# A gated recurrence with a fast-multiplied feed-forward block: how many items of the down product a unit with stored h rows gives out

## The chip, the cores and the metric

The kernel runs on one core of one Trainium2 chip. The metric is device time in microseconds (us) of one execution; smaller is better. Engines: PE is TensorE's matmul side and PEld its weight loads, DVE is VectorE, ACT is ScalarE, POOL is GpSimd, and SP's queue issues most DMAs.

## The reference

```python
S, D, H, Dh, F = 2048, 576, 32, 18, 4608
xn = layernorm(x)
s  = hedgehog_linear_attention(xn, wqkv, w_phi) @ wo
g  = silu(xn @ w_gate)                    # S x F
u  = xn @ w_up                            # S x F
y  = (g * u) @ w_down                     # S x D
out = x + s * silu(y)
```

All is in float32. The attention part comes first in the kernel; the change lies in the last part, the feed-forward block, which takes two thirds of the time.

## The kernel before

**Split operands.** Each float32 operand is held as two parts, hi and lo (`split`, lines 57 to 59: a cast on ACT, a subtraction on DVE), and a product is three matmuls: hi by hi, hi by lo, lo by hi. This is why every prepared operand costs one ACT and one DVE instruction.

**Units.** F = 4608 is cut in 36 blocks f of 128. The token rows are done in two halves, pass 0 (i = 0) and pass 1 (i = 1). A unit (i, n) works on one f of one pass and yields an h block, two tiles of 128 x 512: `ha` (seven buffers) and `hb` (six). In 30 units of each pass, `gate_up` (line 591) computes h from the X operands with seven products of seven matmuls each (128 x 512, line 570), into the PSUM tiles `px`, `py` and `pw`, combined by Strassen's sums. For the other six f, 0 to 5, h was computed in the attention phase and lies in DRAM (`h_dram`); such a unit runs `stored` (line 583), which only loads `ha` and `hb` through SP's queue. Stored units stand at n = 1, 5, 9, 13, 17, 21 in pass 0 and at n = 0, 4, 8, 12, 16, 20 in pass 1.

**The down product.** Four units in a row (n = 4m to 4m + 3) make a group of two pairs. After the third, `strassen` (line 730) puts two steps in a queue, p1 and p7; after the fourth, five more: p4, p5, p6, p2, p3. A step has a preparation (`prep`, line 799: some POOL sums, then two `hh` splits of h rows and two `dw` splits of down weights) and two items. An item (line 785) is 12 matmuls of 128 x 288 (line 669) into one of two PSUM buffers `pd`, then the evacuation, one addition on DVE into a sum tile (line 794; a copy on ACT, line 792, for the first group). The sum tiles have the names `acc`, `X` and `sx`. At the end of a pass two last f pairs are done directly (`plain`), in items of 12 matmuls as well.

**fill and look.** `gate_up` calls `fill` after four of its products, `stored` calls it too. A call gives out items from the head of the queue until `share` units of work (2, later 3) are given; an item of a group with two pairs counts 2, so a call normally gives one. It gives none if no more than `LAG` = 3 units of work are queued. `look` prepares steps up to two ahead. `stored`'s items run with no product of its own between them, and, as one call of `gate_up` comes after its last product, that item stands right before them.

The number of items by unit, worked out from this code, for a middle group of pass 0 and of pass 1 (st is the stored unit; the queue in units of work at the unit's end in brackets):

| pass 0 | n = 7 | n = 8 | n = 9 st | n = 10 |
|---|---|---|---|---|
| before | 4 (22) | 4 (14) | 4 (6) | 2 (10) |

| pass 1 | n = 7 | n = 8 st | n = 9 | n = 10 |
|---|---|---|---|---|
| before | 4 (22) | 4 (14) | 4 (6) | 2 (10) |

At n = 10 the next group's p1 and p7 enter the queue at the unit's end. The four items of n = 9 in pass 0 are the second item of p5, both of p6 and the first of p2; those of n = 10 are the second of p2 and the first of p3. In the stored unit n = 1 of pass 0 the queue is empty. In the first stored unit of pass 1 the calls give out the last items of pass 0.

**Order.** The program text fixes dependences and priorities. A planner, the tile scheduler, orders the instructions on each engine when the program is built, by priority and by its own model of when each will be ready, so an engine's order is near the text's but not the same. At run time each engine follows that fixed order and waits where an operand or a buffer isn't ready.

**Loads.** In pass 0 gate-up weights are loaded raw, split, and written to `w_dram`; in pass 1 the split weights are loaded from there (line 546), each into a buffer that a product of the unit before has freed. At the start of pass 1 the seven X operands are loaded anew (`operands`).

Of the kernel before, what the change touches and what calls it, by code (L numbers as in the profile page):

```python
# [46 lines left out]
def gated_hedgehog_kernel(ctx: ExitStack, tc, x, w_qk, w_v, w_phi, wo, w_gu, w_tail, w_down, ident_in, mask_in, out):  # L47
# [527 lines left out]
    def h_tile():  # L575
        return [fp.tile([P, BT], F32, name=n, bufs=b) for n, b in (("ha", 7), ("hb", 6))]
# [6 lines left out]
    def stored(src, fill):  # L583
        h = h_tile()
        for r in range(2):
            nc.sync.dma_start(h[r], src[:, r * BT:(r + 1) * BT])
        for _ in range(4):
            fill()
        return h

# [255 lines left out]
    def fill(lag=LAG):  # L846
        done = 0
        while queue and done < share[0] and (sum(c for q in queue for c, _ in q[2]) > lag or not queue[0][0]):
            look()
            c, item = queue[0][2].pop(0)  # L850
            item()
            done += c
            if not queue[0][2]:
                queue.pop(0)
# [15 lines left out]
    for i, n, f in units:  # L870
# [3 lines left out]
        if f >= EARLY:  # L874
# [3 lines left out]
            if todo and (i, f) != (0, NF - 1):  # L878
                ready.append(gate_up_weights(*todo.pop(0)))
        h = stored(h_dram[i, f], fill) if f < EARLY else gate_up(w, xo, fill, (i, f) == (0, EARLY))  # L880
        if n % 2 == 0:
            g = {"f": (f, units[units.index((i, n, f)) + 1][2]), "h": [h]}
# [58 lines left out]
```

## Time and profile before

| | |
|---|---|
| median of 3 runs | 1654.41 us (1653.33 to 1656.06) |
| the profiled execution | 1654.66 us, of which the span of instructions is 1652.9 us |
| attention phase and h rows for f below 6 | 0 to about 545 us |
| pass 0 | about 545 to 1086 us |
| pass 1 | about 1086 to 1640 us |
| granted TensorE clock | 0.999 |

In the rows of the profile, L669 PE is an item's matmuls, L570 PE a gate-up product's, L59 DVE the lo half of a split, L58 ACT the hi half, L794 DVE an item's evacuation, L586 SP the loads in `stored`. A timeline row has start, length, engine, line, operation, tiles and shapes and count, and in brackets the engine's idle time before it and what released it. Ends of matmuls are modelled, so time lost on PE is best taken from start to start.

### The profile page before, as it was taken

The page shows a single profiled execution, that of the slowest core. Times are in us where ns is not written, and L with a number is a line of the kernel's source. Part 1 is how long each engine was busy: PE and PEld are TensorE (multiplying, and loading weights), DVE is VectorE, ACT ScalarE, POOL GpSimd, SP SyncE. Part 2 cuts the span into 40 slices and gives each one's busy share as a digit, 9 for nine tenths or more (in the row PEclk, how much of TensorE's full clock was granted, in tenths as well). Part 3 has the DMA queues.
Part 4 walks back from the last instruction along what each step waited for, and adds up shares of the span by engine and source line. Part 5 has one row for each costly group of instructions (what it writes and reads, how often), then busy time and mean ns, then how long its engine had stood idle before and what let it go on. Part 6 is the DMA issues. An engine that isn't in the chain of part 4 may idle for free.

```text
span 1652.9 us, 25205 instructions
## 1 busy us (share of the span) xinstructions
PE 1614.8 (98%) x9441; PEld 1434.1 (87%) x9441; DVE 1175.4 (71%) x1722; ACT 715.7 (43%) x1389; POOL 622.1 (38%) x660
## 2 busy tenths in 40 slices
PE   6999999999999999999999999999999999999998
PEld 5899998999987688888888888888888888888887
DVE  7678758899852477887787777845567667566578
ACT  5533345444431455445444444445433333433334
POOL 3467500343202444554554453422333234133132
PEclk9999999999999999999999999999999999999999
DMA  8623313343218545445445444495444556556435
GB/s 284 215 77 109 109 34 111 94 141 109 73 47 306 182 159 190 158 167 186 161 171 185 174 173 165 132 355 185 152 137 148 164 182 202 171 178 194 139 114 172
DMA packets 118108, 264.69 MB, mean 160 GB/s; under 512 B 12418, under 2 KB 48386, under 8 KB 116194
## 3 DMA queue, kind: packets, MB, share of 16 engines
q1 hardware_dynamic: 107628, 247.44, 44.9%
q0 software_dynamic: 3072, 11.02, 2.4%
q10 hardware_dynamic: 7286, 4.63, 0.9%
q8 instruction: 74, 1.21, 0.3%
q14 instruction: 48, 0.39, 0.1%
HBM read 164.21 MB, written 98.83 MB: 159 GB/s over the span
## 4 chain that ended last, share of the span: by engine, by line
PE 64%; DVE 3%; DMA 1%; issue 1%; POOL 0%; ACT 0%; SPq 0%; DVEq 0%; POOLq 0%
PE px L570 23%; PE pd L669 22%; PE pw L570 11%; PE py L570 6%; PE pe L92 2%; DVE hh L59 1%; DMA ha<-h_dram 1%; DVE acc L641 0%; DVE dw L59 0%; DVE acc L794 0%; DMA X<-s_dram 0%; DMA rb<-in_B_w_down 0%; DVE w L59 0%; DVE X L794 0%; DVE ha L630 0%
## 5 line engine op out<-in xcount | busy, mean ns | idle before, releaser
L669 PEld LDWEIGHTS pd<-dw,hh 128*128 128x128 f32 x3048 | 430.9, 188 | 31.6 <-DVE dw L59 6.4
L669 PE MATMUL pd<-dw,hh 128*128 128x288 f32 x3048 | 448.0, 297 | 8.4 <-DVE dw L59 4.8
L570 PE MATMUL px<-X,w 128*128 128x512 f32 x1440 | 374.8, 394 | 1.8 <-ACT w L58 1.0
L570 PEld LDWEIGHTS px<-X,w 128*128 128x128 f32 x1440 | 261.4, 188 | 55.9 <-ACT s L599 6.1
L570 PE MATMUL pw<-X,w 128*128 128x512 f32 x720 | 186.7, 394 | 0.0
L570 PEld LDWEIGHTS pw<-X,w 128*128 128x128 f32 x720 | 134.0, 189 | 30.2 <-DVE s L604 0.3
L604 DVE TENSOR_TENSOR s<-pw,s 128x512 f32<-128x512 f32 x120 | 82.8, 690 | 105.2 <-ACT s L599 93.4
L92 PE MATMUL pe<-X,wh 128*128 128x512 f32 (+1 forms) x480 | 152.0, 400 | 1.7 <-POOL X L199 0.7
L794 DVE TENSOR_TENSOR acc<-pd,acc 128x576 f32<-128x576 f32 x128 | 96.1, 752 | 72.2 <-PE pd L669 72.0
L599 ACT COPY s<-px 128x512 f32<-128x512 f32 x120 | 70.3, 586 | 156.4 <-PE px L570 156.3
L59 DVE TENSOR_TENSOR hh<-ha,hh 128x512 fp32r<-128x512 f32 x140 | 110.6, 815 | 23.6 <-ACT hh L58 23.0
L58 ACT CAST hh<-ha 128x512 fp32r<-128x512 f32 x140 | 83.1, 620 | 97.2 <-PE pd L669 79.9
L92 PE MATMUL p<-KVWH,X 128*128 128x288 f32 (+1 forms) x640 | 123.6, 298 | 0.9 <-DVE phi L274 0.9
L92 PEld LDWEIGHTS pe<-X,wh 128*128 128x128 f32 (+1 forms) x480 | 88.5, 189 | 19.7 <-DVE h L120 1.5
L766 POOL TENSOR_TENSOR hb<-hb 128x512 f32<-128x512 f32 x34 | 46.1, 1355 | 152.3 <-DVE hb L626 151.8
L92 PEld LDWEIGHTS p<-KVWH,X 128*128 128x128 f32 (+1 forms) x640 | 100.5, 188 | 1.7 <-issue 1.3
L59 DVE TENSOR_TENSOR w<-ld,w 128x512 fp32r<-128x512 f32 (+1 forms) x90 | 76.3, 848 | 34.2 <-ACT w L58 33.2
L753 POOL TENSOR_TENSOR h<-ha,hb 128x512 f32<-128x512 f32 x34 | 45.7, 1344 | 142.6 <-DVE ha L630 101.1
L570 PE MATMUL px<-X,wt 96*128 96x512 f32 x240 | 94.8, 395 | 0.0
L570 PE MATMUL py<-X,w 128*128 128x512 f32 x360 | 93.7, 394 | 0.1
L58 ACT CAST w<-ld 128x512 fp32r<-128x512 f32 (+1 forms) x90 | 49.4, 549 | 83.5 <-POOL ld L560 50.8
L779 POOL TENSOR_TENSOR ha<-ha 128x512 f32<-128x512 f32 x34 | 52.3, 1554 | 80.5 <-DVE hh L59 80.5
(181 smaller groups left out, 3046.9 us busy)
## 6 DMA issues: line engine op xcount, KB each, us to landing
w_dram<-w SPq DMA_DIRECT2D x87, 512.0 KB, 2.8
w<-w_dram SPq DMA_DIRECT2D x87, 512.0 KB, 4.5
wt<-t_dram SPq DMA_DIRECT2D x59, 336.0 KB, 3.4
ld<-in_B_w_gu SPq DMA_DIRECT2D x30, 512.0 KB, 4.4
X<-sum_dram SPq DMA_DIRECT2D x8, 1280.0 KB, 6.6
rt<-in_B_w_down SPq DMA_DIRECT2D x33, 288.0 KB, 3.2
rb<-in_B_w_down SPq DMA_DIRECT2D x33, 288.0 KB, 3.4
w_dram<-w SPq DMA_DIRECT2D x29, 256.0 KB
```

The source lines that it names most:

```text
L58: nc.scalar.copy(hi, src)
L59: nc.vector.tensor_sub(lo, src, hi)
L92: nc.tensor.matmul(ps, l, r, start=n == 0, stop=n == len(pairs) - 1)
L570: nc.tensor.matmul(ps, l, r, start=first and n == 0, stop=last and n == len(mm) - 1, skip_group_check=True)
L599: nc.scalar.copy(t, ps)
L604: nc.vector.tensor_add(t, ps, t)
L669: nc.tensor.matmul(ps, l, r, start=first and n == 0 and m == 0, stop=n == len(hs) - 1 and m == 2, skip_group_check=True)
L753: sub(s, g["h"][0][0], g["h"][0][1])
L766: nc.gpsimd.tensor_add(a21, a21, g["h"][1][1])
L779: sub(a12, a12, g["h"][0][0])
L794: nc.vector.tensor_add(a2, pd[:, :, 0:HALF], a2)
```

## The change

A stored unit calls `fill` twice in place of four times, so it gives out two items where it gave up to four.

```diff
@@ -584,7 +584,7 @@
         h = h_tile()
         for r in range(2):
             nc.sync.dma_start(h[r], src[:, r * BT:(r + 1) * BT])
-        for _ in range(4):
+        for _ in range(2):
             fill()
         return h
```

What is not given out stays in the queue for the calls that follow. By the same counting as above, items and queue become:

| pass 0 | n = 7 | n = 8 | n = 9 st | n = 10 |
|---|---|---|---|---|
| after | 4 (22) | 4 (14) | 2 (10) | 4 (10) |

| pass 1 | n = 7 | n = 8 st | n = 9 | n = 10 |
|---|---|---|---|---|
| after | 4 (22) | 2 (18) | 4 (10) | 4 (10) |

In pass 0 the second item of p6 and the first of p2 move from n = 9 to n = 10. In the first stored unit of pass 1, four items (the last three of the group steps and one of `plain`) are given out in place of six; (1, 1) gives four as before and (1, 2) two where it gave none.

## The prediction

> **What bounds the kernel now.** I read the page first, then who waited for whom on TensorE from 600 us on, then busy time by stretches, and last the timelines around the units that load their h rows.
>
> ```profile
> span 1652.9 us, 25205 instructions
> PE 1614.8 (98%) x9441; PEld 1434.1 (87%) x9441; DVE 1175.4 (71%) x1722; ACT 715.7 (43%) x1389; POOL 622.1 (38%) x660
> PE   6999999999999999999999999999999999999998
> ```
>
> TensorE is busy for 98% of the span. The forecast therefore rests on the few places where it still waits. From 600 to 1056 us, the part of the first pass with a queue to draw on, these are all (us in total, times, longest):
>
> ```profile
> PE pd L669 <- DVE dw L59: 3.3, 3, 1.5
> PE pd L669 <- DVE X L794: 1.9, 4, 0.5
> ```
>
> Busy time by stretches says where they lie. The columns are the length, then PE, weight loads, DVE, ACT and POOL with their counts, the granted clock, and the DMA share and rate.
>
> ```profile
> 600.00:617.00 17.00, 13.74 (x83) 12.08 (x82) 15.75 (x19) 9.27 (x20) 9.96 (x8) 1.00 0.33 104
> 669.38:726.57 57.19, 56.71 (x316) 50.11 (x316) 45.75 (x67) 27.50 (x55) 29.32 (x29) 1.00 0.50 173
> 719.53:726.57 7.04, 6.56 (x50) 6.35 (x48) 6.96 (x11) 2.80 (x6) 4.70 (x4) 1.00 0.60 200
> 726.57:744.42 17.85, 17.85 (x92) 15.33 (x93) 14.79 (x18) 7.87 (x15) 13.43 (x14) 1.00 0.37 122
> 1192.95:1249.58 56.63, 56.63 (x316) 50.15 (x315) 37.88 (x54) 21.51 (x44) 19.25 (x16) 1.00 0.48 147
> 1136.48:1620.00 483.52, 483.52 (x2672) 426.83 (x2670) 316.40 (x458) 187.41 (x370) 150.76 (x124) 1.00 0.52 159
> ```
>
> The third row is a stored unit of pass 0 (n = 9): DVE is busy for 6.96 of 7.04 us there, so DVE ends that stretch, not TensorE. In the gate-up unit behind it (fourth row) DVE has 17.85 - 14.79 = 3.06 us free and TensorE never waits. The last row is nearly all of pass 1: TensorE without an idle moment, its five later stored units included. Four units with a stored one among them take 57.19 us in pass 0 and 56.63 us in pass 1, for the same 316 matmuls: so here a stored unit costs pass 0 about 0.56 us more than it must.
>
> TensorE around that stored unit:
>
> ```profile
> 711.47 1.77 PE L669 MATMUL pd<-dw,hh 128*128 128x288 f32 x12
> 713.08 1.56 PE L570 MATMUL px<-X,w 128*128 128x512 f32 x6
> ...
> 714.71 1.78 PE L669 MATMUL pd<-dw,hh 128*128 128x288 f32 x12
> ...
> 719.53 6.55 PE L669 MATMUL pd<-dw,hh 128*128 128x288 f32 x48
> 726.57 1.82 PE L669 MATMUL pd<-dw,hh 128*128 128x288 f32 x12 [0.48 <-DVE X L794]
> 728.22 1.53 PE L570 MATMUL px<-X,w 128*128 128x512 f32 x6
> ```
>
> One item is 12 matmuls and, from start to start, 713.08 - 711.47 = 1.61 us; the seven matmuls of one gate-up product behind it take 714.71 - 713.08 = 1.63. Five items run in a row, the last of the unit before and the stored unit's four. They need 8.05 us and take 728.22 - 719.53 = 8.69: **0.64 us** are lost (the 0.48 us of idle time is less, because ends of matmuls are modelled). What DVE did meanwhile:
>
> ```profile
> 723.36 0.74 DVE L794 TENSOR_TENSOR acc<-pd,acc 128x576 f32<-128x576 f32 x1
> 724.03 1.72 DVE L59 TENSOR_TENSOR hh<-ha,hh 128x512 fp32r<-128x512 f32 x2
> 725.67 0.75 DVE L794 TENSOR_TENSOR X<-pd,X 128x576 f32<-128x576 f32 x1
> ```
>
> The fifth item needs a pd buffer (there are two), which the third item's addition at 725.67 sets free. That addition stands behind 1.72 us of splits for the next step.
>
> **The change part by part.** It removes the third and fourth call of fill in a stored unit. Nothing is computed less. The two items that these calls gave out go to the next gate-up unit, whose third and fourth calls found the queue at its lag until now; by the code's counts the queue then stands where it stood. (In pass 1 the two items pass through one more unit on the way.) So the change is local: five stored units of pass 0, with 3 items in a row in place of 5, and six of pass 1.
>
> *The four later stored units of pass 0.* The items that waited are the fifth of their runs; they are among those moved, and three in a row need no third evacuation before the products begin. Saved: 4 x 0.64 = 2.6 us. The bounds are 0, if a moved item waits as long at its new place, and 2.6.
>
> *The first of them (n = 5).*
>
> ```profile
> 601.74 3.51 PE L669 MATMUL pd<-dw,hh 128*128 128x288 f32 x25
> 606.17 0.67 PE L669 MATMUL pd<-dw,hh 128*128 128x288 f32 x3 [0.92 <-DVE dw L59]
> 606.68 0.62 PE L570 MATMUL px<-X,w 128*128 128x512 f32 x2
> 608.84 3.46 PE L669 MATMUL pd<-dw,hh 128*128 128x288 f32 x24 [1.54 <-DVE dw L59]
> 613.10 1.36 PE L669 MATMUL pd<-dw,hh 128*128 128x288 f32 x8 [0.80 <-DVE dw L59]
> 614.29 1.07 PE L570 MATMUL px<-X,w 128*128 128x512 f32 x4
> ...
> 607.74 1.04 DVE L59 TENSOR_TENSOR dw<-td,dw 128x288 fp32r<-128x288 f32 x1
> 612.60 0.45 DVE L59 TENSOR_TENSOR dw<-rb,dw 128x288 fp32r<-128x288 f32 x1
> ```
>
> From 601.74 to 614.29 are 12.55 us. The 60 matmuls of the down product need 5 x 1.61 = 8.05, the two of px 2 x 1.63 / 7 = 0.47. Lost: 4.03 us. Items one and two, 24 matmuls, end within the first 25; the third, p6 of the first half, waits at 606.17 and 608.84 for the splits of its own weights, the second of which DVE ends at 608.78. This item stays where it is, so I leave these two waits in. The third wait, for p2's split at 612.60 to 613.05, belongs to a moved item: 613.10 - 608.84 - 2 x 1.61 = **1.04 us**. With the change four products of the next gate-up unit and p6's second half lie ahead of it, 4 x 1.63 + 1.61 = 8.1 us, which cover it. If that cover is gone it costs 1.04 again. Bounds: 0 and 4.03; I take 1.1, the third wait rounded up and so near the lower, because the other two belong to an item that does not move.
>
> *The units that take the two items.* They gain 2 additions on DVE and, earlier or later, the splits of one step (two hh, two dw). Means and extremes over pass 0:
>
> ```profile
> L794 DVE TENSOR_TENSOR acc<-pd,acc 128x576 f32<-128x576 f32 x36 | 27.0, 751 | 9.0 <-PE pd L669 9.0
> L59 DVE TENSOR_TENSOR hh<-ha,hh 128x512 fp32r<-128x512 f32 x36 | 25.2, 730 | 0.0
> L59 DVE TENSOR_TENSOR dw<-rb,dw x8: 448/654/1545, 669.2 to 776.5; 128x288 fp32r<-128x288 f32 x8
> ```
>
> Additions 2 x 0.75 = 1.5, splits between 2 x 0.73 + 2 x 0.45 = 2.4 and 2 x 0.73 + 2 x 1.55 = 4.6: together 3.9 to 6.1 us, against 3.06 us free. But the same work leaves the 7.04 us ahead, where DVE is the last, and TensorE asks for it more slowly: one item per two or so products in place of one after another. Over both stretches DVE is busy for 21.75 of 24.89 us, before and after alike. I take 0 added, with 0.9 to 3.0 us per unit as the other end.
>
> The rows show the same dw split at 0.45 us and at 1.55. The Trainium skill (SBUF — State Buffer, Who interferes with whom) says that a VectorE instruction with two SBUF inputs and a GpSimd instruction that reads SBUF exclude each other, the later one waiting for the earlier one's end. The trace agrees in kind, as POOL is busy for 13.43 of the 17.85 us behind the stored unit; by that rule the moved splits take the longer price there, and the sum would be that of the slower rival below.
>
> *Loads.* The stored unit's ha and hb loads and all weight loads stay the same in number. The rows are first needed by items queued two units later, so a somewhat later start hides; pass 1 has no wait to lose (last row of the stretches), and I put 0 there. At the pass switch there is one load with little slack, a rival below.
>
> The sum: 2.6 + 1.1 = 3.7 us. The profiled execution took 1654.66 us (span 1652.9, the rest around it): 1654.66 - 3.7 = 1650.96. It stood 0.25 us above the median of the runs, 1654.41, so the forecast for that is **1650.7 us**.
>
> **The rivals.** *DVE becomes the bound of the gate-up unit behind (slower).* Place: the first gate-up unit behind each of the five stored units of pass 0. If the moved work has to be done inside it, DVE is 0.9 to 3.0 us over, in the middle 2.0; five times that is 9.8, less the 3.7 that still go: 1654.4 + 6.1 = 1660.5 us. It decides from 0.74 us per unit (3.7 / 5). For it: DVE at 83% and POOL at 75% in that stretch. Against: such units get the work from a stretch that is at 99%, and gate-up units with four items already run there without a wait.
>
> *The pass switch.* The stored unit (1, 0) gives out two items less, so TensorE reaches gate-up (1, 2) 2 x 1.61 = 3.2 us earlier, and its weights are late.
>
> ```profile
> 1102.16 5.55 SPq L546 DMA_DIRECT2D w<-w_dram  x3
> 1110.40 1.54 PE L570 MATMUL pw<-X,w 128*128 128x512 f32 x6
> ...
> DMA to landing us min/median/max: 5.8/6.4/7.1
> ```
>
> The first of three loads, issued at 1102.16, lands at about 1108.6 and serves the product at 1110.40. That product could then stand at 1107.2: up to 1.4 us of new wait (2.1 with the slowest landing), 1650.7 + 1.4 = 1652.1. Against it: TensorE's order there is already not the program's, and the two items can stand ahead of the product.
>
> *The order does not follow.* The planner sets the instruction order itself; if it brings the items back to where they were, or fills their places with others that wait as long, the time is 1654.4.
>
> *All of n = 5 goes.* If the splits of p6 come in time as well, 2.6 + 4.03 = 6.6 us: 1647.8.
>
> **How the numbers follow.** Forecast 0.47 (1649.5 to 1652 by itself), all of n = 5 0.13, pass switch 0.13, order unchanged 0.10, DVE over 0.17. The likeliest is the time, 1650.7. The range 1647.5 to 1658.5 takes in the first four and the lower part of the last. A change of 0.2%, 3.3 us, is about what a measurement of this kernel can tell. Faster by more than that: 0.13 and 0.42 of the 0.47 (its sum is close to the line), 0.55. Within: 0.27, the rest of the forecast, the switch, the order and a trifle of the last. Slower: 0.18.
>
> **What would show it.** In the profile of the changed kernel runs of 36 down-product matmuls stand where 60 stood; the four waits on X L794 are gone, and so is the third of those on dw L59 near 612 us; four-unit periods of pass 0 come to 56.6 us; pass 1 keeps TensorE without idle time. I am wrong if new waits for DVE (dw, hh or a pd evacuation) stand in the first gate-up unit behind a stored one, if that unit's DVE share is near 1, or if TensorE waits for weights near 1107 us.

## The result, and the profile after

The changed kernel takes 1648.54 us (median of 7 runs, 1647.07 to 1649.74), the kernel before 1653.69 us beside it (7 runs). The ratio is 0.9969, with an interval of 0.9959 to 0.9978: some 5.1 us faster, where 3.7 were forecast. The profiled executions have spans of 1647.0 and 1652.9 us; 0.63 us of this difference lie ahead of 601 us, where the two programs are still alike, and are a difference between executions.

Who waited for whom on TensorE from 600 to 1056 us, changed kernel (us in total, times, longest):

```profile
PE pd L669 <- DVE dw L59: 2.5, 2, 1.5
PE pd L669 <- DVE X L794: 0.4, 1, 0.4
```

Three waits on dw have become two. Of the four on X, none is left: the one in this list is another, at 1052 us, which the kernel before has too. TensorE's timeline around the stored units n = 5 and n = 9 of pass 0, changed kernel:

```profile
601.11 3.51 PE L669 MATMUL pd<-dw,hh 128*128 128x288 f32 x25
605.53 0.66 PE L669 MATMUL pd<-dw,hh 128*128 128x288 f32 x3 [0.92 <-DVE dw L59]
606.04 0.62 PE L570 MATMUL px<-X,w 128*128 128x512 f32 x2
608.20 1.33 PE L669 MATMUL pd<-dw,hh 128*128 128x288 f32 x8 [1.54 <-DVE dw L59]
609.36 1.09 PE L570 MATMUL px<-X,w 128*128 128x512 f32 x4
...
660.48 4.97 PE L669 MATMUL pd<-dw,hh 128*128 128x288 f32 x36
665.28 1.55 PE L570 MATMUL px<-X,w 128*128 128x512 f32 x6
```

At n = 5 the first two waits stand as they stood, to the hundredth, and the third has gone with its item. At n = 9 the run has 36 matmuls and takes 4.80 us to the next product, 1.60 for each of three items: nothing is lost. Busy time by stretches. The row of the first fence is the kernel before, from its run at n = 5 to that at n = 9; the first row of the second fence is the same stretch of the changed kernel:

```profile
601.74:662.34 60.60, 57.34 (x316) 50.15 (x315) 46.83 (x65) 31.96 (x64) 29.94 (x28) 1.00 0.46 158
```

```profile
601.11:660.48 59.37, 56.91 (x316) 50.11 (x315) 45.25 (x65) 31.91 (x64) 28.99 (x28) 1.00 0.47 161
660.48:716.86 56.38, 56.38 (x316) 50.16 (x315) 46.68 (x67) 27.33 (x56) 29.24 (x28) 1.00 0.51 175
665.28:683.01 17.73, 17.73 (x99) 15.66 (x98) 17.05 (x20) 7.64 (x16) 14.54 (x15) 1.00 0.43 141
1187.51:1244.03 56.52, 56.52 (x317) 50.19 (x316) 36.50 (x54) 21.61 (x44) 18.84 (x16) 1.00 0.48 147
```

The gain adds up from these rows. The first four-unit period: 60.60 - 59.37 = 1.23 us. The later ones of pass 0: 57.19 - 56.38 = 0.81 us, four times. Those of pass 1: 56.63 - 56.52 = 0.11 us, some five times. Together 5.0 us; the stretch around the pass switch is another 0.25 us shorter (from the wait at 1052 us in the changed kernel to the run at 1131.13 are 78.60 us, in the kernel before 78.85). The third row of the second fence is the gate-up unit that now takes the moved items (n = 10): DVE is busy for 17.05 of 17.73 us, and TensorE does not wait.

### The profile page after: what moved, and what is told of

Read it like the earlier page. It is cut to its first block, busy times and chain, and to the rows that moved or that the text cites. A ratio compares the mean times of both kernels' runs of the same rounds, so it can differ in the third digit from the quotient of the medians.

```text
span 1647.0 us, 25211 instructions
## 1 busy us (share of the span) xinstructions
PE 1613.3 (98%) x9441; PEld 1436.0 (87%) x9441; DVE 1178.3 (72%) x1722; ACT 715.3 (43%) x1389; POOL 618.7 (38%) x660
## 4 chain that ended last, share of the span: by engine, by line
PE 66%; DVE 2%; issue 1%; DMA 0%; POOL 0%; ACT 0%; SPq 0%; DVEq 0%; POOLq 0%
PE pd L669 24%; PE px L570 23%; PE pw L570 11%; PE py L570 6%; PE pe L92 2%; DVE acc L641 0%; DVE hh L59 0%; DMA hb<-h_dram 0%; DMA X<-s_dram 0%; DVE dw L59 0%; DVE w L59 0%; DVE ha L630 0%; DVE acc L642 0%; DVE s L604 0%; DVE acc L824 0%
## 5 line engine op out<-in xcount | busy, mean ns | idle before, releaser
L59 DVE TENSOR_TENSOR hh<-ha,hh 128x512 fp32r<-128x512 f32 x140 | 115.5, 850 | 14.8 <-ACT hh L58 13.8
```

The lines of the kernel that those rows point to most:

```text
L59: nc.vector.tensor_sub(lo, src, hi)
```

## The experiments

Ratios are to the kernel before, run beside each, with 95% intervals. The two calls of the change are written out where a kernel starts from the changed one.

**One pass at a time.**

```diff
-        for _ in range(4):
+        for _ in range(4 if now[0] else 2):     # p0_only: pass 0 only
+        for _ in range(2 if now[0] else 4):     # p1_only: pass 1 only
```

`now` holds the pass and n of the unit.

> Two calls in the stored units of pass 0, four as before in pass 1. Theory A (DVE ends the stored units of pass 0, nothing ends those of pass 1): nearly the whole gain, 4.5 of 5.2 us, ratio about 0.9973. Rival B (every one of the 11 places gains alike because 14 items are dealt out evenly): 5/11 of it, 2.4 us, ratio about 0.9986.

> Four calls in pass 0, two in pass 1. Theory A: 0.7 us, ratio about 0.9996. Rival B: 6/11 of the gain, 2.8 us, ratio about 0.9983.

Measured: 0.9967 (0.9954 to 0.9979) with pass 0 alone and 0.9996 (0.9987 to 1.0005) with pass 1 alone. Both intervals hold theory A's number and leave out rival B's. Nearly all of the gain is pass 0's. What pass 1 gains by itself can't be told from nothing by the times; its trace shows periods some 0.1 us shorter, as in the changed kernel.

**The evacuation first.** The kernel before, the addition of a stored unit's items at high priority:

```diff
-                nc.vector.tensor_add(a2, pd[:, :, 0:HALF], a2)
+                with tc.high_priority() if now[0] == 0 and now[1] % 4 == 1 else ExitStack():
+                    nc.vector.tensor_add(a2, pd[:, :, 0:HALF], a2)
```

> The kernel before with four calls, where the evacuating addition of the items given out in stored units of pass 0 gets high priority, so that DVE does it ahead of the splits of the next step. Theory A1 (the 0.64 us of the four later stored units are the fifth item waiting for a pd buffer behind two splits): these waits go without moving an item, 2.6 us, ratio about 0.9984, unless the splits, now later, make a wait on dw of their own. Rival C (a run of 60 down-product matmuls is slow by itself, whatever DVE does): no change, ratio 1.000.

Measured: 0.9996 (0.9987 to 1.0005). This looks like rival C, and is not. DVE's timeline in this kernel, and TensorE's:

```profile
666.83 1.72 DVE L59 TENSOR_TENSOR hh<-ha,hh 128x512 fp32r<-128x512 f32 x2
668.47 0.75 DVE L795 TENSOR_TENSOR X<-pd,X 128x576 f32<-128x576 f32 x1
...
669.37 1.82 PE L669 MATMUL pd<-dw,hh 128*128 128x288 f32 x12 [0.48 <-DVE X L795]
```

The splits still stand ahead of the addition. A likely reason, which no run here shows, is that priority decides only between instructions that the planner holds ready at the same time, and that the item's matmuls were not yet done when it had the splits at hand. The edit did not make the order that it was to test, so the run says nothing on either theory. The next one takes the DVE work away instead.

**The splits off DVE.** The kernel before, four calls and runs of 60, and for step p2 in the stored units n = 9, 13, 17, 21 of pass 0:

```diff
+        if on_act:      # f is p2 and now[0] == 0 and now[1] in (9, 13, 17, 21)
+            nc.scalar.copy(t[:, 0], src)
+            nc.scalar.copy(t[:, 1], src)
+        else:
             split(t[:, 0], t[:, 1], src)
```

> The kernel before with four calls and runs of 60 matmuls, the same order on TensorE. In the four later stored units of pass 0 the lo part of p2's h rows is a plain copy on ACT in place of the subtraction on DVE (so it holds other values): the 1.72 us of DVE time ahead of the third evacuation are gone. Theory A2 (the 0.64 us are DVE work ahead of that evacuation): the four waits on X L794 go or shrink below 0.1 us, 2.6 us, ratio about 0.9984. Rival C (the long run itself): 8.69 us from the start of the run to the next product as before, ratio 1.000.

Measured: 0.9981 (0.9972 to 0.9990). The kernel leaves out the true lo part of p2's rows. TensorE and DVE around n = 13 in this kernel:

```profile
716.72 8.14 PE L673 MATMUL pd<-dw,hh 128*128 128x288 f32 x60
724.69 1.55 PE L570 MATMUL px<-X,w 128*128 128x512 f32 x6
```

```profile
720.55 0.74 DVE L798 TENSOR_TENSOR acc<-pd,acc 128x576 f32<-128x576 f32 x1
721.72 0.76 DVE L798 TENSOR_TENSOR X<-pd,X 128x576 f32<-128x576 f32 x1 [0.43 <-PE pd L673]
```

DVE now waits for the third item, not the other way round, and the run of 60 takes 7.97 us to the next product in place of 8.69, at all four places alike. Of TensorE's waits on this addition up to 1056 us only the one at 1052 us (0.4 us) is left. Rival C falls: a run of 60 is as fast as five separate items (8.05). The 1.72 us of splits ahead of the third evacuation were the loss, 0.72 us of it each time.

**How many calls.** Three, one and none, by the number in the loop.

> Three calls in place of four. Only the last item of each run moves. Theory A: that is the item that waits, in all five stored units of pass 0, so nearly all of the gain comes already: 3.7 to 4.6 us, ratio 0.9972 to 0.9978. Rival B (evenness): half, 2.6 us, ratio about 0.9984.

> One call in place of four: 13 calls for the 14 items of a group, so one item more stays queued after each group. Theory A (what matters is that no third item follows in the run that DVE has to evacuate in time): no more gain than two calls, ratio 0.9965 to 0.9975. Rival D (the h rows are held too long: with a fourth part of the next group's items behind, the seven ha buffers run out): new waits in the gate-up units, ratio above 0.9990.

> No call at all in stored units: 12 calls for 14 items, the backlog grows by two items a group to about ten. Theory A without a limit from buffers: like one call, ratio about 0.997. Rival D: the ha and hb buffers run out, gate-up units wait for items and the backlog ends in a long run without products at the pass switch; slower than two calls by 2 to 10 us, ratio 0.998 to 1.003.

Measured: three calls 0.9970 (0.9958 to 0.9982), one 0.9991 (0.9981 to 1.0001), none 0.9983 (0.9975 to 0.9992). Three calls are as good as two: only the last item of a run had to go, as theory A has it, and half the gain for half the items is out. One call gives most of the gain back, so rival D's direction is right, and none lies in the range that rival D gave for it, though its interval overlaps that of two calls a little. In the trace with one call the cause is another than the one that I named. TensorE's waits from 600 us with one call, and one of them followed back (POOL, ACT and TensorE in order of time):

```profile
PE py L570 <- ACT py L611: 5.0, 3, 2.7
```

```profile
727.27 1.84 SPq L727 DMA_DIRECT2D rb<-in_B_w_down  x2
730.30 0.81 POOL L754 TENSOR_TENSOR td<-rb,rt 128x288 f32<-128x288 f32 x1 [1.90 <-DMA rb<-in_B_w_down]
...
735.70 0.73 POOL L560 TENSOR_TENSOR ld<-ld,ts 128x256 f32<-128x256 f32 x1
...
736.47 0.41 ACT L58 CAST w<-ld 128x256 fp32r<-128x256 f32 x1 [4.32 <-POOL ld L560]
...
737.96 0.57 ACT L611 COPY py<-px 128x512 f32<-128x512 f32 x1
...
738.59 1.73 PE L570 MATMUL py<-X,w 128*128 128x512 f32 x6 [1.93 <-ACT py L611]
```

The next group's down rows `rb` are loaded only from 727.27 on, into buffers that the late p3 held: 16.5 us behind the start of the stored unit's run, where the changed kernel has 7.7. POOL's sums on them come first in its order, then the sum for gate-up weights (line 560); ACT waits for that one with a cast and has the copy into py behind it; TensorE waits for the copy. So items put off too long reach TensorE through POOL's and ACT's fixed orders. That the h buffers ran out isn't seen in this chain. The other waits of these two kernels weren't followed back. The intervals of one call and of none overlap, so it stays open whether none is the better of the two.

**More DVE work in the unit behind.** The changed kernel, where in the first gate-up unit behind a stored one of pass 0 the splits of a step are computed twice or five times:

```diff
     def split(hi, lo, src, twice=False):
         nc.scalar.copy(hi, src)
-        nc.vector.tensor_sub(lo, src, hi)
+        for _ in range(1 + twice):              # splits_five: range(1 + 4 * twice)
+            nc.vector.tensor_sub(lo, src, hi)
```

> The changed kernel, where in the first gate-up unit behind each stored one of pass 0 every lo part of an hh or dw split is computed twice with the same result: about 8 more subtractions of 0.45 to 0.73 us, some 5 us of DVE time in a unit of 17.7 us in which DVE is busy for 17.05 already. If the rival of the prediction (DVE becomes the bound of that unit) is only just out of reach: 5 units x about 4 us = up to 20 us slower, ratio up to 1.009 against before. If the splits there are done well ahead of their use (theory A): DVE catches up in the next unit, which has 3.8 us free, and at most 1 us per unit is lost, ratio 0.997 to 1.000.

> The changed kernel, where the splits of steps prepared in the first gate-up unit behind a stored one of pass 0 are computed five times (computing them twice put only four more subtractions there, not eight, as one step is prepared in that unit): 16 more subtractions, about 9 to 10 us of DVE time per group of four units, against 56.4 - 46.7 = 9.7 us that DVE has free there. Theory A3 (DVE has its free time at its disposal because splits are made well ahead): 0 to 2 us lost per group, at most 10 in all, ratio 0.997 to 1.003. The prediction's rival (what isn't done inside that unit is lost): the unit has 0.7 us free, so 8 to 9 us per group, over 40 in all, ratio above 1.02.

Measured: twice 0.9968 (0.9955 to 0.9981), five times 1.0148 (1.0134 to 1.0162). One step is prepared in that unit, so twice means four more subtractions, not the eight of the first expectation. With them DVE is full and TensorE still doesn't wait in it (a four-unit period takes 56.6 us in place of 56.4, which the time doesn't show):

```profile
663.92:681.60 17.68, 17.68 (x99) 15.61 (x98) 17.68 (x23) 7.65 (x16) 13.05 (x13) 1.00 0.42 139
```

With 16 more a four-unit period takes 727.92 - 666.33 = 61.6 us (starts of two runs of 36) in place of 56.4. TensorE's timeline:

```profile
666.33 4.97 PE L670 MATMUL pd<-dw,hh 128*128 128x288 f32 x36
...
686.44 1.65 PE L571 MATMUL pw<-X,w 128*128 128x512 f32 x6 [0.63 <-DVE s L605]
...
697.10 2.93 PE L571 MATMUL py<-X,w 128*128 128x512 f32 x6 [2.15 <-ACT py L612]
...
700.25 1.68 PE L571 MATMUL px<-X,w 128*128 128x512 f32 x6
...
727.92 4.97 PE L670 MATMUL pd<-dw,hh 128*128 128x288 f32 x36
```

The loss, 5.2 us per group, lies between the two theories' 0 to 2 and 8 to 9. Part of the free time of later units does serve as cover (A3), but products also wait, 0.63 us at 686.44 for DVE itself and 2.15 us at 697.10 for ACT, behind which the next seven matmuls take 1.5 us longer than usual (last section). What ACT was late for, POOL and ACT in order of time:

```profile
681.25 4.54 POOL L755 TENSOR_TENSOR td<-rb,rt 128x288 f32<-128x288 f32 x1 [6.09 <-DMA rb<-in_B_w_down]
...
695.64 0.41 ACT L58 CAST w<-ld 128x256 fp32r<-128x256 f32 x1 [5.01 <-POOL ld L561]
```

This is the chain seen with one call: late `rb` rows (the splits that read the old ones are computed five times), POOL's sums, ACT's cast, the copy. One of POOL's sums takes 4.54 us, where the chain above has 0.81; why was not tested. By this trace, then, some 3.6 of the 5.2 us (the wait of 2.15 and the slow matmuls behind it) come by that way, and 0.63 from DVE directly; the rest was not taken apart. In the first group DVE's own wait is longer, 4.9 us at 626.61. Extra DVE work begins to cost somewhere between 4 and 16 subtractions more than the change brings.

**The first items of the pass.** The changed kernel without a call at n = 5 (`first_none`), and in addition without the first of the four calls at n = 3 (`first_two_later`):

```diff
+        for _ in range(0 if now == [0, 5] else 2):
...
         product(wp, w, 4, S1, True, False)
-        fill()
+        if now != [0, 3]:
+            fill()
```

> The changed kernel with no call in the first stored unit of pass 0 that has a queue (n = 5), two in the others. The two waits left there, 0.92 and 1.54 us for the splits of p6, then have four products of the next unit ahead of them. Theory A: both go, 2.5 us less than the changed kernel, ratio about 0.9954. Rival: DVE, slowed by POOL in that stretch, is late for the next item just the same, ratio as the changed kernel, 0.9969.

> The changed kernel with no call at n = 5 of pass 0, and at n = 3 the first of gate_up's four calls left out, so that the first items of the pass (p1) come one product pair later; three items are given there as before. The 1.53 us that TensorE waits at about 573 us for their dw split should go as well: 1.5 us less than without a call at n = 5 alone, ratio about 0.9942. Rival: other first waits take its place (weights on ACT, 0.5 us each), ratio 0.9951.

Measured: 0.9951 (0.9939 to 0.9963) and 0.9955 (0.9942 to 0.9967). The former has the lowest time here, 1646.54 us, though the two intervals hold each other's number; its profile from 600 to 1620 us has neither of the two waits on dw, and one new one:

```profile
PE py L570 <- ACT py L611: 0.6, 1, 0.6
PE pd L669 <- DVE X L794: 0.4, 1, 0.4
```

The second edit gains nothing more. The 1.53 us for dw at 573 us are gone, and TensorE waits for the copy out of px instead, as no item lies between two products that share it:

```profile
576.08 1.65 PE L570 MATMUL px<-X,w 128*128 128x512 f32 x6 [2.18 <-ACT s L599]
```

## Why the prediction was right, step by step

**What bounds the kernel.** Right in the main: most of the gain lies in the few waits that were listed, and pass 0 has nearly all of it (`p0_only`, `p1_only`). Some 0.8 us come from pass 1 and the switch, where no wait was listed.

**The four later stored units.** Mechanism right, and shown by taking the splits away with the long run left in place: 8.69 us became 7.97. The term was sized too small: 4 x 0.64 = 2.6 us, where the four periods give 4 x 0.81 = 3.2. I took 1.61 us for an item of a long run; the undisturbed run of 60 needs 7.97 / 5 = 1.59, so 0.72 us were lost, not 0.64. The other 0.09 us of each period were not taken apart. Pass 1 has 0.11 us per period, which the forecast set at 0 and whose cause wasn't looked into. The stretch at 719.53 that the prediction calls n = 9 is n = 13 (n = 9 starts at 662.34 and loses the same).

**n = 5.** Right in each part: 1.23 us gained against 1.1, of which the third wait had been sized at 1.04 and the rest was not taken apart; the third wait gone, the first two left at 0.92 and 1.54 us. `first_none` shows why they stayed: it moves the item itself, and they go.

**The units that take the items.** Right that nothing is added. But a DVE share near 1 there was named as a sign of being wrong, and it stands at 17.05 of 17.73 us while TensorE waits for nothing: much of that work is preparation ahead of need. The longer prices of the splits did come there (dw splits of 1.06 and 1.07 us at 673 and 675 us, against 0.45), and the slower time that the rival drew from them did not. `splits_twice` fills the unit and costs nothing that the time shows, `splits_five` does cost. The price of that rival, whatever isn't done inside the unit, was too simple: the free time of the next units covers a part, and much of what `splits_five` lost came through POOL and ACT.

**The pass switch.** It cost nothing, but by a narrow margin. A run of 24 down-product matmuls stands ahead of the rival's load in both kernels. In the kernel before:

```profile
1091.06 3.46 PE L669 MATMUL pd<-dw,hh 128*128 128x288 f32 x24
```

TensorE and SP in the changed kernel:

```profile
1085.91 3.46 PE L669 MATMUL pd<-dw,hh 128*128 128x288 f32 x24
...
1096.60 4.77 SPq L546 DMA_DIRECT2D w<-w_dram  x3
...
1102.68 1.55 PE L570 MATMUL pw<-X,w 128*128 128x512 f32 x6
```

All of this stands 5.15 us earlier in the changed kernel, so times are to be counted from that run. The first of the three loads is issued 11.10 us behind it in the kernel before and 10.69 us in the changed one (10.73 with pass 0 alone changed): it stayed nearly where it was, as the rival had it. The product stands 19.34 us behind it before and 16.77 after, so it came 2.6 us earlier, where the rival took 3.2. From issue to product 6.08 us are left, and the product doesn't wait. The landings shown for the kernel before, 5.8 to 7.1 us, would have made a wait of up to 1.0 us, so that none appeared is partly luck.

**The order.** TensorE's order followed the program: runs of 36 where 60 and 48 + 12 stood.

**The number.** Forecast 3.7 us, measured 5.1 between the medians, 5.0 from the rows: 0.6 too little for the four units, 0.1 for n = 5, 0.6 for the later periods of pass 1. Of the 2.2 us between the forecast time, 1650.7, and the measured 1648.54, 0.7 are the kernel before itself, whose median was 1654.41 then and 1653.69 beside the result. The chances have a slip: slower got 0.18, though the one rival that is slower had 0.17 in all.

## What to carry to other kernels

Where one engine is at 98%, look for short stretches in which it has no work but that of a slower helper, and put other work between: one item less in a run of five was already enough. Idle time in a list of waits can understate the loss where ends are modelled (0.48 us listed, 0.72 lost); measure the loss from start to start, against an undisturbed run of the same work. A helper at full share did no harm here as long as what it did was ahead of need, and work put off too long can come back through the fixed order of engines that seem to have nothing to do with it.

## What the runs showed of the hardware

A wait of about 2 us on TensorE cost more than its length. Granted clock (last column but two) with the splits five times:

```profile
690.00:697.00 7.00, 4.96 (x26) 3.89 (x24) 4.36 (x6) 1.99 (x6) 6.83 (x8) 1.00 0.27 109
697.00:700.50 3.50, 3.40 (x8) 2.72 (x9) 3.50 (x9) 1.55 (x4) 1.60 (x2) 0.52 0.20 75
700.50:708.00 7.50, 7.50 (x43) 6.61 (x43) 5.92 (x9) 4.21 (x9) 3.22 (x4) 1.00 0.52 179
```

Behind the wait of 2.15 us the clock is 0.52 for some 3 us, and the next seven matmuls take 700.25 - 697.10 = 3.15 us in place of 1.63: 1.5 us on top of the wait. In the kernel with one call, behind the wait of 1.93 us at 738.59, the mean clock from 738 to 743 us is 0.70, and the seven matmuls from 740.54 on take 2.96 us. Behind the 1.54 us at 608.20 in the changed kernel nothing of the kind is seen (8 matmuls and the next start within 1.16 us). The Trainium skill (TensorE: Matmul & The Clock Gate, Part 1: The HAM clock gate) describes a clock that is halved after an idle window and restored after a busy one, windows of about 3.4 us that run freely. The trace agrees with the halving and roughly with the time to recover; here an idle time shorter than such a window was enough.
